# A fused attention and convolution-gate kernel: bias added by the matmul unit, reciprocals folded into the transposes, and eight-plus-eight first taps moved from GpSimd to ScalarE

## Chip, cores and metric

One core of one Trainium2 chip. The metric is the device time of one execution in microseconds. Three executions of the kernel before took 440.35, 440.97 and 441.27 us; their median is 440.97 us.

## What is computed

Attention over 4 batches, 8 heads, 768 positions and head size 64, with eight global keys and a local window of 96 keys behind each query, an ALiBi-like bias, and then a gated feed-forward block on the result:

```python
scores = scale * np.matmul(q, k.transpose(0, 1, 3, 2))
keep = is_global | is_local
bias = -slopes[:, None, None] * dist[None, :, :]
scores = np.where(keep, scores + bias[None, :, :, :], -1000000000.0)
scores = scores - np.max(scores, axis=-1, keepdims=True)
a = np.exp(scores)
a = a / (np.sum(a, axis=-1, keepdims=True) + 1e-09)
x = np.matmul(a, v)                      # then heads side by side: 768 x 512
h = np.maximum(x @ w_in, 0.0)            # 512 -> 1024
conv_out = sum(conv_w[k] * hp[:, k:k + S, :] for k in range(3))
out = (h * (1 / (1 + np.exp(-conv_out)))) @ w_out   # 1024 -> 512
```

## The kernel before, in words

The attention is cut into 32 jobs, one for each batch, half `u` of the 768 positions and pair of heads. A job has three blocks of 128 queries, so there are 96 steps `s`; twelve steps make a half. Each step treats two heads (`j`) and sees 232 gathered keys (128 in the first block of a sequence). A step goes through these stages:

- `scores` (L369): one f32 matmul for each head into one PSUM bank (L381) in the first twelve jobs, that is steps 0 to 35; later jobs use two single-pass matmuls for each head (L391).
- `maxima` (L400): on VectorE, one custom instruction for each head (L408) adds the bias from the bf16 table `tab`, scales, writes the sum back into PSUM and keeps the row extreme; a small accumulator read follows each.
- `exps` (L415): two exponentials on ScalarE (L425) into `pbuf`, with the row sums.
- `normalise` (L433), not in steps 0 to 11, which are scaled later: adds an epsilon, takes a reciprocal on VectorE (L437) and multiplies the 128x232 rows in place, on GpSimd (L443) or partly on ScalarE (L441). In steps 14 to 29 (`alone`) the epsilon (L436) and both multiplications are on GpSimd.
- `transposes` (L445): four PE transposes (L450, L452) with the f32 identity as the moving operand, evacuated by ScalarE (L455).
- `values` or `block`: the value matmuls (L501), then the split into high and low parts (L513, L517).

The feed-forward part of a half (`ffn`, L663) is a queue of items filled in between the steps: 24 `mm1` items (L539), evacuated with a ReLU by ScalarE (L549); the convolution `conv` (L578), whose first tap is a GpSimd multiplication (L585) and whose other two taps are VectorE instructions (L586, L587); the gate (L605, L616), a split (L638 to L641), and `mm2` (L652).

Steps 0 to 13 are ordered by hand (`by_hand`, L792): each engine runs in the order that the code writes, with `warm` filler matmuls on the PE (L168) and one or two pieces of weight decoding on VectorE (L311, L313, L324) for each step. From step 14 the framework orders each engine's instructions itself, from priorities and a cost model, and `fill` (L724) hands out a share of the queue at each step. The weight decoding is spread over steps up to about 30. SP issues the loads, in order.

PSUM has two buffers for scores, two for transposes, one for values and three for the feed-forward products. `setup`, a scratch tile of the start, and the query tiles from job 12 on share one buffer, with the tag `rq`.

Of the kernel before, what the change touches and what calls it, by code (L numbers as in the profile page):

```python
# [9 lines left out]
F32 = mybir.dt.float32  # L10
F32R = mybir.dt.float32r
BF16 = mybir.dt.bfloat16
I32 = mybir.dt.int32
U32 = mybir.dt.uint32
AF = mybir.ActivationFunctionType
ALU = mybir.AluOpType
# [4 lines left out]
P = 128  # L21
# [4 lines left out]
NB = TB // P  # L26
NPREV, NGLOB = 96, 8
WIN = NPREV + P + NGLOB
# [7 lines left out]
NU, SPU = 2 * B, NPAIR * NB  # L36
# [4 lines left out]
HAND = 14  # L41
# [19 lines left out]
def key_start(u, i):  # L61
    return (P + NGLOB) * i - (0 if u or i == 0 else P + NGLOB - 32)
# [5 lines left out]
def fast_path(tc, io):  # L68
    nc = tc.nc
    V, A, G, T = nc.vector, nc.scalar, nc.gpsimd, nc.tensor  # L70
# [4 lines left out]
    def pool(name, bufs, **kw):  # L75
        p = tc.tile_pool(name=name, bufs=bufs, **kw)
        pools.append(p)
        return p.__enter__()

    const = pool("const", 1)  # L80
    p1 = pool("p1", 1)
# [105 lines left out]
    G.iota(keyi, pattern=[[1, 64]], base=0, channel_multiplier=0)  # L187
    ident = const.tile([P, P], F32, name="ident")
    make_identity(nc, ident)
    V.tensor_copy(rel, reli)  # L190
    keepkey = p1.tile([P, NT + 64], F32, tag="ob", name="keep")
    keep, key = keepkey[:, :NT], keepkey[:, NT:]
# [12 lines left out]
    tab = const.tile([P, H, NT], BF16, name="tab")  # L205
# [151 lines left out]
        V.tensor_tensor(bad, bad, red[:, 1:2], ALU.add)  # L357

    steps = [(m, i) for m in range(len(jobs)) for i in range(NB)]
    last_ttr = {}  # L360
    st_s, st_pt, pv, xt, sums = {}, {}, {}, {}, {}

    def alone(s):
        return HAND <= s < NB * (NATIVE - 2)

    def free(s):
        return s < NB * FREE

    def scores(s):  # L369
        m, i = steps[s]  # L370
        b, u, hp = jobs[m]
        w = NKC[u]
        first = u == 0 and i == 0
        n = W0 if first else WIN
        k0 = key_start(u, i)
        both = ps_s.tile([P, 2, 256], F32, tag="s", name=f"s{s}")
        sp = [both[:, 0], both[:, 1]]
        for j in range(2):
            if m < NATIVE:
                rq, rk = raw[m]  # L380
                last_mm[s] = T.matmul(  # L381
                    sp[j][:, :n],
                    rq[:, j, i * P : (i + 1) * P],
                    rk[:, k0 : k0 + n],
                    start=True,
                    stop=True,
                )
                continue
            qh, ql, kk = qk[m]
            for n_, (q_, st, sp_) in enumerate(((qh, True, False), (ql, False, True))):  # L390
                last_mm[s] = T.matmul(  # L391
                    sp[j][:, :n],
                    q_[:, j * TB + i * P : j * TB + (i + 1) * P],
                    kk[:, j * w + k0 : j * w + k0 + n],
                    start=st,
                    stop=sp_,
                )
        st_s[s] = (sp, n, first)

    def maxima(s):  # L400
        m, i = steps[s]
        b, u, hp = jobs[m]
        sp, n, first = st_s[s]
        mm = p1.tile([P, 8], F32, tag="mm", name=f"mm{s}", bufs=6)
        for j in range(2):
            h = 2 * hp + j
            tb = tab[:, h, WIN:] if first else tab[:, h, 0:WIN]
            last_ttr[s] = V.tensor_tensor_reduce(  # L408
                out=sp[j][:, :n], in0=sp[j][:, :n], in1=tb,
                scale=-0.125, scalar=3.0e38, op0=ALU.add, op1=ALU.min,  # L410
                accum_out=mm[:, j : j + 1],
            )
        st_s[s] = (sp, n, mm)

    def exps(s):  # L415
        m, i = steps[s]
        sp, n, mm = st_s[s]
        pb = pbuf[s % NPB]
        total = mm[:, 2:4]
        if free(s):  # L420
            if i == 0:
                sums[m] = p1.tile([P, 4 * NB], F32, tag="sum", name=f"sum{m}", bufs=2)
            total = sums[m][:, 2 * i : 2 * i + 2]
        for j in range(2):
            last_exp[s] = A.activation(  # L425
                pb[:, j * WIN : j * WIN + n], sp[j][:, :n], AF.Exp,
                bias=mm[:, j : j + 1], scale=-1.0, accum_out=total[:, j : j + 1],
            )
        st_s[s] = (pb, n, mm)
        if s < SHARED and not alone(s) and not free(s):  # L430
            A.activation(mm[:, 4:6], mm[:, 2:4], AF.Identity, bias=eps)

    def normalise(s):  # L433
        pb, n, mm = st_s[s]
        if s >= SHARED or alone(s):
            (G if alone(s) else V).tensor_scalar(mm[:, 4:6], mm[:, 2:4], 1.0e-9, 1.0, ALU.add, ALU.mult)  # L436
        V.reciprocal(mm[:, 6:8], mm[:, 4:6])  # L437
        for j in range(2):
            x, inv = pb[:, j * WIN : j * WIN + n], mm[:, 6 + j : 7 + j]
            if j and s < SHARED and not alone(s):  # L440
                A.activation(x, x, AF.Copy, scale=inv)  # L441
            else:
                G.tensor_scalar(x, x, inv, 1.0, ALU.mult, ALU.mult)  # L443

    def transposes(s):  # L445
        m, i = steps[s]
        pb, n, _ = st_s.pop(s)
        pt = ps_t.tile([P, 2, 2, P], F32, tag="t", name=f"t{s}")
        for j in range(2):
            T.transpose(pt[:, 0, j], pb[:, j * WIN : j * WIN + P], ident)  # L450
            if n > P:
                T.transpose(pt[:, 1, j], pb[:, j * WIN + P : j * WIN + 256], ident)  # L452
        sb = p2.tile([P, 2, 2, P], F32, tag="pt", name=f"pt{s}", bufs=NPT)
        k = 2 if n > P else 1
        last_ev[s] = A.activation(sb[:, :k], pt[:, :k], AF.Copy)  # L455
        st_pt[s] = sb
# [121 lines left out]
    def conv(n, f):  # L578
        t0, t1 = bounds[n % 2]
        w = t1 - t0  # L580
        if f == 0:
            cbuf[n] = p1.tile([P, NF, S - CB], F32, tag="c", name=f"c{n}")
        c = cbuf[n][:, f, :w]
        tap = lambda k: (hbuf[:, f, t0 + k : t1 + k], cw[:, k * NF + f : k * NF + f + 1])
        G.tensor_scalar(c, *tap(1), 1.0, ALU.mult, ALU.mult)  # L585
        V.scalar_tensor_tensor(c, *tap(0), c, ALU.mult, ALU.add)  # L586
        V.scalar_tensor_tensor(c, *tap(2), c, ALU.mult, ALU.add)  # L587

# [5 lines left out]
    ready, sure, exact = set(), set(), []  # L594
# [68 lines left out]
    def ffn(n, defer=True):  # L663
# [4 lines left out]
        for f in range(NF):  # L668
            for part in range(3):
                if n or f >= EARLY or not begun[0]:  # L670
                    add(1, mm1, n, f, part)
                elif part == 0:
                    for k in range(begun[0], NK):
                        add(1, mm1_slice, f, k)
                if part == 1:
                    if early:
                        items.append(early.pop(0))
                    if f >= lag:
                        add(0, conv, n, f - lag)
                if part == 2:  # L680
                    g = f - lag + 1
                    if g > 0 and g % WG == 0:
                        add(0, gate, n, g // WG - 1)
                    g -= 1
                    if g > 0 and g % WG == 0:
                        add(0, saturated, n, [g // WG - 1])
        old = tiles_of(n - 1) if n else []
        post = [(0, conv, (n, f)) for f in range(NF - lag, NF)] + [(0, gates, (n,))]
        post += [(0, saturated, (n, range(NG)))]
        post += [(0, split, (n, t)) for t in parts_of(n)]  # L690
# [31 lines left out]
    last_exp, last_mm, last_ev = {}, {}, {}  # L722
# [69 lines left out]
    def by_hand(s):  # L792
        m, i = steps[s]
        p, q = s - 1, s - 2
        scores(s)
        if q >= 0 and free(q):
            block(*steps[q])
# [6 lines left out]
        if p >= 0 and free(p):  # L804
            transposes(p)
        maxima(s)
        exps(s)
        if ends(s - 3):
            mixed_low((s - 3) // NB)
# [5 lines left out]
        if p >= 0 and not free(p):  # L815
            normalise(p)
# [14 lines left out]
    for s in range(len(steps) + LAG_V + 1):  # L831
# [4 lines left out]
        else:  # L836
# [5 lines left out]
            if s < len(steps):  # L842
                scores(s)
                maxima(s)
                exps(s)
# [12 lines left out]
            if s <= len(steps):  # L858
                normalise(s - 1)
# [6 lines left out]
            if s < len(steps) + LAG_T and not free(s - LAG_T):  # L866
                transposes(s - LAG_T)
# [185 lines left out]
def build(nc, io):  # L1053
    with tile.TileContext(nc, schedule_with_timeline_sim=True) as tc:
        fast_path(tc, io)
# [51 lines left out]
```

## Time and profile before

| | |
|---|---|
| median of three executions | 440.97 us |
| the profiled execution | 440.63 us |
| its span, first to last instruction | 438.8 us |
| outside the span | 1.8 us |
| granted TensorE clock | 1.0 of full speed throughout |
| steps 14 to 23, by ScalarE's exponentials | from 45.2 to about 76 us |

Busy times are those of one engine. PE is the matmul unit, PEld its weight loads, which overlap the matmuls, DVE is VectorE, ACT ScalarE, POOL GpSimd. A matmul's end is modelled, so the distance between the starts of two matmuls says more of the PE than the length of either. The chain of waits is followed back from the last instruction: a piece of it is time that, at that moment, the end waited for.

### The profile page before, as it was taken

How to read it: one execution, taken by the hardware profiler on the slowest of the kernel's cores; microseconds unless marked ns; L12 is line 12 of the kernel's file. 1: busy time of each engine (PE TensorE's matmuls, PEld its weight loads, DVE VectorE, ACT ScalarE, POOL GpSimd, SP SyncE). 2: the span in 40 equal slices, each digit the busy share in tenths (PEclk: the TensorE clock that was granted, in tenths of full speed). 3: DMA queues.
4: the chain of work that ended last, by engine and by line, in shares of the span. 5: the costliest groups of instructions: out<-in, count | busy, mean ns of one | idle time of the engine just before them, and what ended most of it. 6: DMA issues, size and time to landing. Idle time of an engine off the chain costs nothing.

```text
span 438.8 us, 10010 instructions
## 1 busy us (share of the span) xinstructions
PE 427.0 (97%) x3566; PEld 404.6 (92%) x3566; DVE 345.1 (79%) x894; ACT 285.2 (65%) x771; POOL 225.4 (51%) x324
## 2 busy tenths in 40 slices
PE   9899979999999999999999999999999999999996
PEld 8677967889999999999999999999999999999996
DVE  6797899979999988767989797867999868556500
ACT  2778688597797866647885767647885866136311
POOL 4312789955735963557668843557668631022000
PEclk9999999999999999999999999999999999999999
DMA  8876864322245234353354224442243467800111
GB/s 256 269 229 183 257 176 154 83 83 91 92 122 160 80 111 136 104 176 94 105 150 152 51 101 134 149 141 85 92 162 120 124 242 240 271 26 0 49 50 55
DMA packets 22570, 58.77 MB, mean 134 GB/s; under 512 B 2928, under 2 KB 6256, under 8 KB 22512
## 3 DMA queue, kind: packets, MB, share of 16 engines
q1 hardware_dynamic: 18608, 51.56, 37.7%
q10 hardware_dynamic: 3904, 6.49, 4.1%
q8 instruction: 30, 0.49, 0.5%
q14 instruction: 28, 0.23, 0.2%
HBM read 51.75 MB, written 6.29 MB: 132 GB/s over the span
## 4 chain that ended last, share of the span: by engine, by line
PE 78%; DVE 12%; ACT 6%; issue 2%; POOL 1%; ACTq 0%; DVEq 0%; POOLq 0%
PE o L652 27%; PE h L539 25%; PE pv L501 7%; PE s L391 5%; PE t L450 4%; PE t L452 3%; DVE s L408 3%; PE s L381 3%; ACT pbuf L425 3%; PE warm L168 2%; DVE c L587 2%; DVE c L586 1%; PE o L922 1%; ACT pt L455 1%; DVE w L313 1%
## 5 line engine op out<-in xcount | busy, mean ns | idle before, releaser
L443 POOL TENSOR_SCALAR pbuf<-pbuf,mm 128x232 f32<-128x232 f32 (+1 forms) x156 | 112.3, 732 | 65.1 <-DVE mm L437 41.0
L425 ACT ACTIVATE pbuf<-s,mm 128x232 f32<-128x232 f32 (+1 forms) x192 | 83.0, 440 | 51.8 <-DVE mm L408 38.1
L408 DVE CUSTOM_DVE_ANT_0 s<-s,tab 128x232 f32<-128x232 f32 (+1 forms) x192 | 73.1, 381 | 9.8 <-PE s L391 4.8
L652 PE MATMUL o<-woh,gh 128*128 128x256 f32 x368 | 77.2, 288 | 0.0
L652 PE MATMUL o<-wol,gh 128*128 128x256 f32 x368 | 76.1, 282 | 0.0
L585 POOL TENSOR_SCALAR c<-hbuf,cw 128x382 f32<-128x382 f32 (+1 forms) x64 | 46.1, 723 | 57.8 <-ACT hbuf L549 55.1
L652 PE MATMUL o<-woh,gl 128*128 128x256 f32 x368 | 72.9, 279 | 0.0
L455 ACT ACTIVATE pt<-t 128x512 f32<-128x512 f32 (+1 forms) x96 | 53.7, 566 | 15.0 <-PE t L452 11.5
L539 PE MATMUL h<-xh,wih 128*128 128x384 f32 x252 | 58.2, 348 | 0.3 <-ACT ob L658 0.2
L539 PE MATMUL h<-xl,wih 128*128 128x384 f32 x252 | 58.0, 345 | 0.0
L652 PEld LDWEIGHTS o<-wol,gh 128*128 128x128 f32 x368 | 57.2, 189 | 0.7
L652 PEld LDWEIGHTS o<-woh,gh 128*128 128x128 f32 x368 | 56.6, 189 | 0.7
L539 PE MATMUL h<-xh,wil 128*128 128x384 f32 x252 | 56.7, 344 | 0.0
L652 PEld LDWEIGHTS o<-woh,gl 128*128 128x128 f32 x368 | 56.2, 189 | 0.1
L586 DVE SCALAR_TENSOR_TENSOR c<-hbuf,cw,c 128x382 f32<-128x382 f32 (+1 forms) x64 | 45.2, 712 | 13.4 <-POOL c L585 13.0
L450 PE MATMUL t<-ident,pbuf 128*128 128x128 f32 x192 | 47.6, 276 | 0.9 <-POOL pbuf L443 0.9
L539 PEld LDWEIGHTS h<-xh,wih 128*128 128x128 f32 x252 | 43.4, 189 | 1.4 <-ACT x L484 0.5
L539 PEld LDWEIGHTS h<-xh,wil 128*128 128x128 f32 x252 | 43.8, 188 | 0.6
L549 ACT ACTIVATE hbuf<-h 128x384 f32<-128x384 f32 x64 | 31.2, 492 | 20.2 <-PE h L539 20.1
L587 DVE SCALAR_TENSOR_TENSOR c<-hbuf,cw,c 128x382 f32<-128x382 f32 (+1 forms) x64 | 43.4, 681 | 0.5
L539 PEld LDWEIGHTS h<-xl,wih 128*128 128x128 f32 x252 | 43.3, 189 | 0.3
L501 PE MATMUL pv<-pt,v 128*64 128x128 f32 (+1 forms) x664 | 40.9, 268 | 0.9 <-ACT pt L455 0.9
(123 smaller groups left out, 844.6 us busy)
## 6 DMA issues: line engine op xcount, KB each, us to landing
v<-in_vv SPq DMA_DIRECT2D x32, 384.0 KB, 3.7
wr<-in_w SPq DMA_DIRECT2D x16, 512.0 KB, 4.4
check<-in_w SPq DMA_DIRECT2D x16, 512.0 KB, 4.1
rq<-in_qk SPq DMA_DIRECT2D x20, 384.0 KB, 3.2
rk<-in_qk SPq DMA_DIRECT2D x12, 504.0 KB, 4.0
out<-ob ACTq DMA_DIRECT2D x23, 256.0 KB, 2.5
rk<-in_qk SPq DMA_DIRECT2D x8, 400.0 KB, 3.6
qz<-in_qt SPq DMA_DIRECT2D x22, 96.0 KB, 4.7
```

The source lines that it names most:

```text
L408: last_ttr[s] = V.tensor_tensor_reduce(out=sp[j][:, :n], in0=sp[j][:, :n], in1=tb, scale=-0.125, scalar=3.0e38, op0=ALU.add, op1=ALU.min, ...
L425: last_exp[s] = A.activation(pb[:, j * WIN : j * WIN + n], sp[j][:, :n], AF.Exp, bias=mm[:, j : j + 1], scale=-1.0, accum_out=total[:, j : ...
L443: G.tensor_scalar(x, x, inv, 1.0, ALU.mult, ALU.mult)
L450: T.transpose(pt[:, 0, j], pb[:, j * WIN : j * WIN + P], ident)
L455: last_ev[s] = A.activation(sb[:, :k], pt[:, :k], AF.Copy)
L501: T.matmul(pv[m][64 * j : 64 * j + 64, i * P + q : (i + 1) * P], vt[m][:n, i, c, 64 * j : 64 * j + 64], sb[:n, c, j, q:], start=c == 0, st ...
L539: T.matmul(ps[:, :TB], w_[:, k, fs], x_, start=part == 0 and k == 0, stop=part == 2 and k == NK - 1,)
L549: A.activation(half, ps[:, :TB], AF.Relu, scale=0.5)
L585: G.tensor_scalar(c, *tap(1), 1.0, ALU.mult, ALU.mult)
L586: V.scalar_tensor_tensor(c, *tap(0), c, ALU.mult, ALU.add)
L587: V.scalar_tensor_tensor(c, *tap(2), c, ALU.mult, ALU.add)
L652: T.matmul(ps[:, c], g_[:, f], w_[:, f, c], start=f == part == k == 0, stop=f == NF - 1 and part == 2 and k == 1,)
```

## The change

Three edits. In steps 3 to 23 the bias table is added in PSUM by a further matmul for each head, with a bf16 identity as the stationary operand; VectorE then takes the row maxima of both heads in one reduction, followed by a small scaling. In steps 14 to 23 the rows of `pbuf` are no longer multiplied: GpSimd multiplies the 128x128 identity by the reciprocals, and the four transposes become ordinary f32 matmuls with that diagonal as the moving operand. In halves 0 and 1 the first tap of the convolution is a ScalarE copy with a scale.

```diff
+    ident16 = const.tile([P, P], BF16, name="ident16")
+    G.tensor_copy(ident16, ident)
...
+    def added(s):
+        return NB <= s < 2 * SPU
+    def spun(s):
+        return HAND <= s < 2 * SPU
...
-                    stop=True,
+                    stop=not added(s),
                 )
+                if added(s):
+                    c0 = WIN if first else 0
+                    last_mm[s] = T.matmul(
+                        sp[j][:, :n], ident16, tab[:, 2 * hp + j, c0 : c0 + n], start=False, stop=True
+                    )
...
+        if added(s):
+            st_s[s] = (sp, n, mm)
+            both = whole.pop(s)
+            V.tensor_reduce(mm[:, 2:4], both[:, :, :n], axis=mybir.AxisListType.X, op=ALU.max)
+            last_ttr[s] = V.tensor_scalar(mm[:, 0:2], mm[:, 2:4], -0.125, None, ALU.mult)
+            return
...
-                bias=mm[:, j : j + 1], scale=-1.0, accum_out=total[:, j : j + 1],
+                bias=mm[:, j : j + 1], scale=0.125 if added(s) else -1.0,
+                accum_out=total[:, j : j + 1],
...
+        if spun(s):
+            if not scale:
+                scale["all"] = p1.tile([P, 3, 2, P], F32, tag="rq", name="scale")
+            scale[s] = scale["all"][:, s % 3]
+            for j in range(2):
+                G.tensor_scalar(scale[s][:, j], ident, mm[:, 6 + j : 7 + j], 1.0, ALU.mult, ALU.mult)
+            return
...
-            T.transpose(pt[:, 0, j], pb[:, j * WIN : j * WIN + P], ident)
-            if n > P:
-                T.transpose(pt[:, 1, j], pb[:, j * WIN + P : j * WIN + 256], ident)
+            for c in range(2 if n > P else 1):
+                x = pb[:, j * WIN + c * P : j * WIN + (c + 1) * P]
+                if spun(s):
+                    T.matmul(pt[:, c, j], x, scale[s][:, j], start=True, stop=True)
+                else:
+                    T.transpose(pt[:, c, j], x, ident)
...
-        G.tensor_scalar(c, *tap(1), 1.0, ALU.mult, ALU.mult)
+        if n < 2 and not exact:
+            A.activation(c, tap(1)[0], AF.Copy, scale=tap(1)[1])
+        else:
+            G.tensor_scalar(c, *tap(1), 1.0, ALU.mult, ALU.mult)
```

## Rows read from the trace of the kernel before

**Rows 1.** The page: weight loads and matmuls in 40 slices, tenths busy.
```profile
PE   9899979999999999999999999999999999999996
PEld 8677967889999999999999999999999999999996
```

**Rows 2.** The page: chain that ended last, share of the span by engine.
```profile
PE 78%; DVE 12%; ACT 6%; issue 2%; POOL 1%; ACTq 0%; DVEq 0%; POOLq 0%
```

**Rows 3.** Busy time by stretch: PE, PEld, DVE, ACT, POOL, then clock and DMA.
```profile
15.00:45.00 30.00, 28.73 (x276) 22.81 (x276) 25.52 (x92) 23.11 (x75) 7.60 (x13) 1.00 0.74 215
45.00:76.00 31.00, 27.93 (x207) 24.75 (x207) 28.94 (x83) 24.75 (x72) 26.76 (x38) 1.00 0.63 198
76.00:92.00 16.00, 14.52 (x110) 12.70 (x105) 14.84 (x46) 10.89 (x39) 15.01 (x26) 1.00 0.37 108
92.00:140.00 48.00, 47.44 (x375) 44.99 (x374) 44.16 (x94) 40.88 (x111) 23.96 (x30) 1.00 0.32 102
200.00:300.00 100.00, 100.00 (x851) 97.07 (x850) 83.49 (x220) 68.37 (x184) 63.59 (x82) 1.00 0.38 117
```

**Rows 4.** Chain of waits, 56 to 76 us: start, length, engine and line.
```profile
59.01 0.78 DVE c L587
59.79 0.88 DVE c L586
60.67 0.32 DVE s L408
60.99 0.06 DVE mm L408
...
61.38 0.60 DVE c L587
```

**Rows 5.** PE in order of time, 61 to 67 us, with waits in brackets.
```profile
63.49 1.05 PE L381 MATMUL s<-rk,qz 128*128 128x232 f32 x4 [1.45 <-ACT pbuf L425]
...
65.93 0.33 PE L452 MATMUL t<-ident,pbuf 128*128 128x128 f32 x1 [0.59 <-POOL pbuf L443]
```

**Rows 6.** Chain of waits in the hand-ordered steps, 7 to 48 us.
```profile
20.27 0.46 PE s L381 x4
20.73 0.62 ACT pt L455
...
22.73 0.35 PE warm L168 x6
...
23.31 0.11 PE t L450
...
31.14 0.79 PE s L381 x4
```

**Rows 7.** Groups by line and shape: count, busy us, mean ns, idle before.
```profile
L408 DVE CUSTOM_DVE_ANT_0 s<-s,tab 128x232 f32<-128x232 f32 x160 | 63.7, 399 | 7.6 <-PE s L391 3.7 <-ACT pt L455 1.4 <-PE s L381 1.0
L408 DVE DVE_READ_ACCUMULATOR2_ANT mm<- 128x1 f32 x192 | 26.4, 137 | 0.1
L349 DVE TENSOR_REDUCE misc<-acc 128x1 f32<-128x512 f32 x1 | 0.7, 685 | 0.0
L242 DVE TENSOR_REDUCE misc<-misc 128x1 f32<-128x3 f32 x1 | 0.2, 157 | 0.0
L436 DVE TENSOR_SCALAR mm<-mm 128x2 f32<-128x2 f32 x56 | 13.9, 248 | 16.8 <-ACT pbuf L425 16.5
L443 POOL TENSOR_SCALAR pbuf<-pbuf,mm 128x232 f32<-128x232 f32 x134 | 100.5, 761 | 47.6 <-DVE mm L437 27.4 <-ACT pbuf L425 8.4 <-ACT pt L455 4.3
L443 POOL TENSOR_SCALAR pbuf<-pbuf,mm 128x128 f32<-128x128 f32 x22 | 11.9, 551 | 17.5 <-DVE mm L437 13.6 <-PE pv L501 1.4 <-PE o L652 1.2
L441 ACT ACTIVATE pbuf<-pbuf,mm 128x232 f32<-128x232 f32 x10 | 4.8, 486 | 0.0
L549 ACT ACTIVATE hbuf<-h 128x384 f32<-128x384 f32 x64 | 31.2, 492 | 20.2 <-PE h L539 20.1
```

**Rows 8.** First tap L585 on POOL by stretch: busy us and count.
```profile
45.00:92.00 47.00, 6.87 (x8) 1.00 0.54 167
92.00:140.00 48.00, 6.90 (x8) 1.00 0.32 102
```

More of the change, by code (lines that the diff above doesn't have):

```diff
@@ L359, in fast_path @@
     steps = [(m, i) for m in range(len(jobs)) for i in range(NB)]
-    last_ttr = {}
+    last_ttr, scale, whole = {}, {}, {}
     st_s, st_pt, pv, xt, sums = {}, {}, {}, {}, {}
+    def added(s):
+        return NB <= s < 2 * SPU
     def alone(s):
         return HAND <= s < NB * (NATIVE - 2)
+    def spun(s):
+        return HAND <= s < 2 * SPU
     def free(s):
@@ L398, in scores @@
         st_s[s] = (sp, n, first)
+        if added(s):
+            whole[s] = both
     def maxima(s):
@@ L404, in maxima @@
         mm = p1.tile([P, 8], F32, tag="mm", name=f"mm{s}", bufs=6)
+        if added(s):
+            st_s[s] = (sp, n, mm)
[3 more added lines that the diff above has]
+            return
         for j in range(2):
```

## The prediction

> **What bounds the kernel now.** I read the page's slices first [rows 1]: from the tenth slice on, the weight loads stand at 9 tenths and the matmuls too; before that the loads dip to 6 to 8 tenths. Then the chain that ended last [rows 2]: 78% of it is PE. So the end is set by the PE's work plus the time in which the PE starved, and the starving lies in the first 140 us.
>
> The table by stretch [rows 3] says how much. Matmul busy time hides short waits, because ends are modelled; the weight loads dip where the waits are, so I measure with them. In the full stretch from 200 to 300 us they are busy 97.07 of 100. By that yardstick, 45 to 76 us could hold 31 x 0.971 = 30.1 us of loads and holds 24.75: 5.35 us of slack. 76 to 92 us: 15.53 - 12.70 = 2.83. 92 to 140 us: 46.6 - 44.99 = 1.6. Together 9.8 us can be won at most behind 45 us, and whatever PE work is added there has to come out of the same 9.8.
>
> Why does it starve between 45 and 76 us? There VectorE is busy 28.94 of 31 us and GpSimd 26.76 [rows 3], the chain runs through VectorE piece after piece [rows 4], and the PE's waits name ScalarE's exponentials (which wait for the maxima) and GpSimd's row multiplications [rows 5]. Two loaded engines feed a PE that is itself nearly loaded. Ahead of 45 us the order is written by hand; the chain [rows 6] passes through PE pieces (transposes, scores, filler) with an evacuation on ScalarE between them.
>
> **Part 1, the bias on the PE, steps 3 to 23.** Added: 21 steps x 2 bf16 matmuls, 232 columns wide (128 in steps 3, 6 and 9). No such matmul is in the trace. The nearest row is the bf16 filler of 128 columns, 0.35 us for 6, 58 ns each [rows 6], a floor. The ceiling is an f32 score instruction of 232 columns, 0.79 us for 4, 197 ns [rows 6]. The filler scaled by 232/128 gives 105 ns, and I take 0.1 us, nearer the filler since both are bf16: 0.2 us a step. That is 2.0 us in steps 14 to 23 (bounds 1.2 to 3.9) and, with three narrow steps at 0.12, 8 x 0.2 + 3 x 0.12 = 2.0 us in steps 3 to 13.
>
> Removed on VectorE: two custom instructions with their reads, 2 x (0.32 + 0.06) = 0.76 us of the chain where another instruction lies between [rows 4], about 1.05 by lengths (2 x (399 + 137) ns, [rows 7]) where they stand next to each other. Added: a reduction of 464 elements. The two reductions in the trace, 685 ns for 512 elements and 157 for 3 [rows 7], give 157 + 461 x 1.037 = 635 ns, and the scaling of two elements is at most 248 ns [rows 7], 0.1 to 0.2 in the chain. About 0.75 to 0.85 us. I take a gain of 0.1 us a step, 1 us over steps 14 to 23; the ends are nothing and 0.25 us a step. The Trainium skill (VectorE: DVE Perf Modes, Rules for kernel authors) speaks against this exchange: a reduction runs at one element per cycle, is called the slowest VectorE operation, and one is told to keep the count of operations low. The row agrees as to the rate (1.04 ns an element), and by that rule alone VectorE's term would be 0 in place of 1 us.
>
> In the hand-ordered steps the 2.0 us are not all on the path. Of steps 4 to 13, seven (4 to 10) have their scores in the PE part of the chain: 5 x 0.2 + 2 x 0.12 = 1.2 us. At two of them the next thing is a wait for an evacuation that is late for another reason (0.62 us of L455 behind 0.46 us of scores, [rows 6]), so about 0.4 is absorbed. Behind the matmul that waits or lengthens, the PE queue holds value matmuls and filler. VectorE's earlier end gives back 0.2. Sum: +0.6 us (bounds -0.5 and +2.0). The identity's bf16 copy on GpSimd is one 128x128 operation, at most 0.55 us [rows 7]; it stands ahead of GpSimd's wait for VectorE's first distances and costs nothing; without that cover, 0.55. The bias table becomes an operand of the PE rather than of VectorE; it is written two or more steps ahead, so no new wait.
>
> **Part 2, the diagonal, steps 14 to 23.** Removed on GpSimd: 20 multiplications at 761 ns; added: 20 at 551 (same operation, 128 columns, [rows 7]): -4.2 us. On the PE, a transpose is one instruction, 0.11 us [rows 6]; an f32 matmul is two, as the four score instructions of a step with two heads show: 128 columns take 0.46 / 4 = 0.115 each [rows 6]. So four transposes go from 0.44 to 0.88-0.92 us: +0.44 a step, **+4.4 us** over ten steps. This term has a narrow bound (4 to 5). The reciprocal tile shares the buffer of `rq`: its first write waits for readers of step 6, long past; the query load of job 12, on SP, waits for step 23's transposes but is issued only in step 31. No DMA is added.
>
> **Part 3, the first tap.** 16 GpSimd instructions go, 6.87 us in 45 to 92 and 6.90 in 92 to 140 us [rows 8]. 16 ScalarE copies come. Nearest rows: the scaled copy of 232 columns, 486 ns, and a ReLU of 384 columns, 492 ns [rows 7]; between 0.49 and 0.62 us each, I take 0.5 net of overlap: 4 us in each of the two stretches. ScalarE is busy 24.75 + 10.89 of 47 us and 40.88 of 48 [rows 3]; it rises to 39.6 of 47 and 44.9 of 48. No queue is at its limit, so I cost it at nothing on its own; the cover is thin in the second stretch (rival 2).
>
> **The sum.** PE work added between 45 and 76 us: 2.0 + 4.4 = 6.4 us. Slack there: 5.35. GpSimd loses about a third of its load and VectorE about 1 us, so most starving should go, but the added work exceeds the slack: the PE becomes the bound of these ten steps. I let it recover 4.3 of 5.35 there, 0.7 of 2.83 in 76 to 92 us (whose waits follow from GpSimd's arrears) and nothing after. Net: 6.4 - 5.0 = +1.4. With the hand-ordered +0.6 and 0.2 for ScalarE: **+2.2 us**. Against the profiled execution's own 440.63 us (span 438.8 plus 1.83 around it): 442.8 us. That execution lies 0.3 us below the median of three, so against the median it is +1.9.
>
> **Rival 1: faster, because the feeding engines were the real limit.** The same VectorE instruction takes 0.60 us in one place and 0.78 in another, its neighbour 0.88 [rows 4], while GpSimd was busy 26.76 of 31 us [rows 3]. If those lengths come from the two working at once, taking 6.87 + 4.2 us off GpSimd shortens some 25 VectorE instructions by up to 0.2 us each, and all starving behind 45 us but 1 us is won: 6.4 - 8.8 = -2.4, +0.6 by hand: 438.8 us. It decides once recovery passes 7 us. The Trainium skill (GPSIMD Engine Reference, Specifications) has such a rule: GpSimd's way into SBUF is shared with VectorE, with contention when a VectorE instruction reads two SBUF inputs, as the two later taps do. By that rule, which the two lengths bear out, the time is this rival's. Against it: the recovery would have to reach stretches that the added work does not touch. Chance 0.25.
>
> **Rival 2: ScalarE takes over.** Between 92 and 140 us ScalarE has the exponentials, evacuations, ReLUs and gates of a half, and 44.9 of 48 us would be full. A tap between a ReLU and the next exponential delays that exponential by 0.5 us; if half of the 16 do, +4 less what the forecast holds for it: 446.6 us. For it: the waits for exponentials [rows 5]. Against: the PE has a backlog of feed-forward work there, and its loads are near the yardstick. Chance 0.13.
>
> **Rival 3: the parts cancel.** Recovery of 6 to 7 us pays for the added 6.4 and the hand-ordered 0.6: 440.1 to 441.8 us, 440.9 in the middle. Chance 0.17. That the edits don't do what they say I can't construct; the shared buffer is the only place for it.
>
> **Numbers.** A measurement of this kernel can tell about 0.2%, 0.9 us, from no change. Forecast 442.8 us, chance 0.45 (441.9 to 445). Faster 0.25, within 0.2% 0.17, slower 0.45 + 0.13 = 0.58. The range runs from 438.4 (rival 1 with a little more) to 446.6 (rival 2), leaving out about 0.1 on each side; the bias price's bounds (-1 to +3 us about the forecast, [rows 6]) lie inside. The slower cases alone: 441.9 to 446.6.
>
> **What would show it.** Right: in the ten steps the weight loads rise from 0.80 of the time to 0.93 or more, GpSimd falls to about half, the chain there turns from VectorE to PE, four diagonal transposes take 0.9 us, a bias matmul 0.1, and the steps end 1 to 3 us later than at 76 us. Wrong: the chain stays on VectorE with the loads still at 0.8; step 24 begins before 75 us; ScalarE over 0.93 busy with the PE waiting for it; or a bias matmul at 0.2 us.

## The result, and the profile after

Five executions of the changed kernel have a median of 443.64 us (443.32 to 444.49), five of the kernel before 440.46 us. The ratio is 1.0075 [1.0064, 1.0085]: slower by about 3.2 us, inside the range, 0.84 us above the forecast. The profiled execution took 443.32 us, its span 441.4 against 438.8.

The page of the changed kernel: busy times, the slices that answer to [rows 1], and the shares of the chain that answer to [rows 2].

```profile
PE 432.4 (98%) x3648; PEld 410.7 (93%) x3648; DVE 341.3 (77%) x852; ACT 291.8 (66%) x787; POOL 212.1 (48%) x309
PE   9999999999999999999999999999999999999996
PEld 8777998889999999999999999999999999999996
PE 80%; DVE 6%; DMA 5%; ACT 4%; issue 2%; POOL 2%; ACTq 0%; POOLq 0%; DVEq 0%
```

VectorE's share of the chain halves, from 12% to 6%, and PE's grows by 2 points, to 80%. A DMA share of 5% is new; it is taken up below.

By stretch, the changed kernel, columns as in [rows 3]; the stretches are moved by one to three microseconds so that they hold the same steps:

```profile
46.00:78.00 32.00, 32.00 (x260) 29.26 (x260) 27.82 (x66) 27.06 (x79) 21.46 (x36) 1.00 0.57 174
78.00:94.00 16.00, 14.57 (x110) 12.74 (x106) 13.80 (x45) 11.48 (x38) 10.97 (x21) 1.00 0.46 133
94.00:143.00 49.00, 49.00 (x388) 47.30 (x386) 43.85 (x101) 46.48 (x128) 20.48 (x21) 1.00 0.35 102
```

In the first stretch the loads rise from 0.80 to 29.26 / 32 = 0.91, GpSimd falls from 0.86 to 0.67 and VectorE from 0.93 to 0.87. In the second, where no PE work was added, the loads are as before (12.74 of 16 us against 12.70). ScalarE is fullest in the third, 0.95, but the PE's loads there are at 47.30 / 49 = 0.965, close to the yardstick of 0.971: it has work to put before the exponentials.

The changed kernel's PE in order of time, in one of the ten steps:

```profile
60.12 0.66 PE L389 MATMUL s<-rk,qz 128*128 128x232 f32 x2
60.61 0.26 PE L398 MATMUL s<-tab,ident 128*128 128x232 bf16 x1
60.71 0.57 PE L389 MATMUL s<-rk,qz 128*128 128x232 f32 x2
61.11 0.26 PE L398 MATMUL s<-tab,ident 128*128 128x232 bf16 x1
61.21 1.07 PE L482 MATMUL t<-scale,pbuf 128*128 128x128 f32 x8
```

Read the starts, not the lengths. A bias matmul at 61.11 is followed at 61.21: 0.10 us, as costed. One diagonal transpose is two instructions. And the chain of the changed kernel for the same ten steps, which answers to [rows 4]:

```profile
61.38 0.90 PE t L482 x8
62.28 0.69 PE h L571 x4
62.97 0.89 PE t L482 x8
...
67.36 0.11 PE s L398
67.50 0.64 DVE mm L423
68.38 1.66 POOL scale L465 x2
70.12 0.20 POOL mm L458
70.35 0.17 DVE mm L459
70.52 0.88 DVE c L621
```

Eight diagonal instructions take 0.89 to 0.90 us, against 0.44 for four transposes: the 0.44 us a step of the prediction. Up to 67 us the chain is on the PE, as forecast; from there on it runs through VectorE and GpSimd. The PE does not starve beside it in these steps: it is busy 31.45 of 31.45 us (row under e5). What this part of the chain leads to lies behind step 24, where the PE is busy 14.99 of 16.42 us (77.58 to 94.00).

Groups of the changed kernel by shape, which answer to [rows 7] and [rows 8]:

```profile
L423 DVE TENSOR_REDUCE mm<-s 128x2 f32<-128x464 f32 x18 | 11.4, 634 | 4.0 <-PE s L398 4.0
L424 DVE TENSOR_SCALAR mm<-mm 128x2 f32<-128x2 f32 x21 | 3.7, 176 | 0.5
L465 POOL TENSOR_SCALAR scale<-ident,mm 128x128 f32<-128x128 f32 x20 | 15.3, 775 | 4.4 <-DVE mm L459 3.0 <-PE t L482 0.7 <-DVE mm L424 0.7
L618 ACT ACTIVATE c<-hbuf,cw 128x382 f32<-128x382 f32 x8 | 4.9, 631 | 0.0
L398 PEld LDWEIGHTS <-ident 128*128 128x128 bf16 x42 | 4.1, 98 | 0.2
```

The reduction takes 634 ns (635 estimated) and the scaling 176. The diagonal's multiplication takes 775 ns, not 551. The prices of GpSimd in these steps, 45 to 77 us before and 45 to 78 after, are:

```profile
L443 POOL TENSOR_SCALAR pbuf<-pbuf,mm 128x232 f32<-128x232 f32 x17 | 14.3, 854 | 0.3
```

```profile
L465 POOL TENSOR_SCALAR scale<-ident,mm 128x128 f32<-128x128 f32 x19 | 15.0, 797 | 4.4 <-DVE mm L459 3.0 <-PE t L482 0.7 <-DVE mm L424 0.7
```

The replaced multiplication took 854 ns here, not the 761 of the whole kernel, so an instruction saves about 0.06 to 0.08 us in place of 0.21. GpSimd is relieved almost by the taps alone. A tap on ScalarE takes 631 ns, a little above the bracket of 0.49 to 0.62.

**Where the 2.6 us of span arise.** Four marks cut the execution: an exponential of the hand-ordered start (at 13.80 us before, 13.84 after), the first of step 14, the first of step 57, and the start of ScalarE's last evacuation (L926 before, L961 after); the end is that of the last instruction, 438.83 and 441.43 us. Before / after:

| stretch | before | after | difference |
|---|---|---|---|
| start mark to step 14 | 31.44 | 32.29 | +0.85 |
| step 14 to step 57 | 158.95 | 159.58 | +0.63 |
| step 57 to the last evacuation | 231.04 | 232.11 | +1.07 |
| last evacuation to the end | 3.61 | 3.61 | 0 |

The first two terms are those that the prediction has. The third it has not. The chain of the changed kernel there:

```profile
359.39 1.02 DVE acc L344
360.42 0.02 issue
360.44 4.44 DMA check<-in_w
364.87 0.02 issue
364.90 0.70 DVE acc L344
365.60 0.02 issue
365.62 4.52 DMA check<-in_w
370.14 0.03 issue
...
370.24 0.69 DVE acc L344
370.93 1.15 DVE c L673
```

These are the loads (16 of 512 KB) of weight words whose top bits VectorE gathers into `acc` (L341, L344), for the choice between this program and its general branch; a further load is issued when an earlier one has been read. The gate's split (L673) stands behind the last of them on VectorE. In the kernel before the chain of this stretch is on the PE throughout.

### The profile page after: what moved, and what is told of

It is laid out like the page before. It is cut to its first block, busy times and chain, and to the rows that moved or that the text cites. A ratio compares the mean times of both kernels' runs of the same rounds, so it can differ in the third digit from the quotient of the medians.

```text
span 441.4 us, 10130 instructions
## 1 busy us (share of the span) xinstructions
PE 432.4 (98%) x3648; PEld 410.7 (93%) x3648; DVE 341.3 (77%) x852; ACT 291.8 (66%) x787; POOL 212.1 (48%) x309
## 4 chain that ended last, share of the span: by engine, by line
PE 80%; DVE 6%; DMA 5%; ACT 4%; issue 2%; POOL 2%; ACTq 0%; POOLq 0%; DVEq 0%
PE h L571 26%; PE o L687 25%; PE pv L533 7%; PE t L484 6%; PE s L404 5%; DMA check<-in_w 5%; PE s L389 4%; PE warm L168 2%; ACT pbuf L446 2%; PE o L957 1%; DVE s L429 1%; PE t L482 1%; DVE c L621 1%; ACT pt L487 1%; POOL scale L465 1%
## 5 line engine op out<-in xcount | busy, mean ns | idle before, releaser
L472 POOL TENSOR_SCALAR pbuf<-pbuf,mm 128x232 f32<-128x232 f32 (+1 forms) x136 | 98.1, 732 | 76.0 <-DVE mm L459 53.0
L429 DVE CUSTOM_DVE_ANT_0 s<-s,tab 128x232 f32<-128x232 f32 (+1 forms) x150 | 56.9, 382 | 9.5 <-PE s L404 7.5
L620 POOL TENSOR_SCALAR c<-hbuf,cw 128x382 f32<-128x382 f32 (+1 forms) x48 | 32.5, 679 | 54.3 <-ACT hbuf L581 33.1
L621 DVE SCALAR_TENSOR_TENSOR c<-hbuf,cw,c 128x382 f32<-128x382 f32 (+1 forms) x64 | 45.2, 709 | 10.6 <-POOL c L620 9.8
L484 PE MATMUL t<-ident,pbuf 128*128 128x128 f32 x312 | 50.7, 274 | 0.8 <-ACT pt L487 0.4
L533 PEld LDWEIGHTS pv<-pt,v 128*64 128x64 f32 (+1 forms) x664 | 34.0, 136 | 9.4 <-ACT pt L487 4.6
```

Of the source, the lines that this page charges most:

```text
L429: last_ttr[s] = V.tensor_tensor_reduce(out=sp[j][:, :n], in0=sp[j][:, :n], in1=tb, scale=-0.125, scalar=3.0e38, op0=ALU.add, op1=ALU.min, ...
L484: T.transpose(pt[:, c, j], x, ident)
L533: T.matmul(pv[m][64 * j : 64 * j + 64, i * P + q : (i + 1) * P], vt[m][:n, i, c, 64 * j : 64 * j + 64], sb[:n, c, j, q:], start=c == 0, st ...
```

## The experiments

Each kernel ran beside the kernel before on the same chip. The table gives the differences from the kernel before, in us: the stretches from each kernel's profiled execution, the last column from the medians. "Recovered" is the PE work added in steps 14 to 23, at 0.2 us a step for the bias and 0.44 for the diagonal, less the difference of step 14 to 57 (in e11 1.1 us come on top for steps 24 to 26, of which step 24 is narrow); it is what came, on balance, out of the pool of starved time that the prediction put at 9.8 us.

| kernel | PE work added | to step 14 | 14 to 57 | recovered | 57 to last evacuation | last evacuation to end | median |
|---|---|---|---|---|---|---|---|
| changed | 6.4 | +0.85 | +0.63 | 5.8 | +1.07 | 0 | +3.2 |
| e1, taps | 0 | +0.01 | -1.02 | 1.0 | 0 | 0 | -0.9 |
| e2, bias | 2.0 | +0.84 | +0.70 | 1.3 | -0.15 | +0.47 | +2.2 |
| e3, diagonal | 4.4 | +0.01 | -0.93 | 5.3 | +0.58 | +0.91 | +1.0 |
| e4, all but bias by hand | 6.4 | -0.02 | +0.68 | 5.7 | 0 | 0 | +0.9 |
| e5, taps and diagonal | 4.4 | 0 | -3.02 | 7.4 | 0 | +1.30 | -1.8 |
| e6, bias by hand | 0 | +0.84 | -0.21 | 0.2 | 0 | 0 | +0.8 |
| e7, three check loads | 6.4 | +0.83 | +0.69 | 5.7 | 0 | +0.36 | +2.1 |
| e8, bias twice | 8.4 | +0.86 | +1.33 | 7.1 | -0.30 | 0 | +2.7 |
| e9, zero matmuls on e5 | 6.4 | -0.02 | -0.54 | 6.9 | 0 | +0.13 | -0.2 |
| e10, reduction on e5 | 4.4 | +0.20 | -4.44 | 8.8 | +0.20 | +1.03 | -3.3 |
| e11, e5 to step 26 | 5.5 | 0 | -0.91 | 6.4 | 0 | 0 | -0.8 |
| e12, e5 with half 0's taps | 4.4 | +0.02 | -2.05 | 6.5 | 0 | +1.77 | -0.5 |

The four stretches add up to the median's difference within 0.4 us, but for e8 (0.8 off) and the changed kernel (0.6); of both the profiled execution is the fastest of five, 0.4 and 0.3 us under its median.

**Parts alone.** All edits are against the changed kernel. e1 keeps the taps only:

```diff
 def added(s):
-    return NB <= s < 2 * SPU
+    return False
...
 def spun(s):
-    return HAND <= s < 2 * SPU
+    return False
```

> Only the first tap of halves 0 and 1 moves to ScalarE; bias and transposes as before. Theory (the cost is added PE work, the taps only relieve GpSimd and VectorE): no PE work is added, so the time falls by 0.5 to 2 us against before, and the steps behind 45 us end earlier. Rival (ScalarE takes over between 92 and 140 us): slower than before by 1 to 4 us. Rival (taps don't matter): within 0.5 us.

439.35 us, ratio 0.9978 [0.997, 0.9987]. The taps gain 0.9 us, as expected, and by the traces all of it in the ten steps (30.55 to 29.56 us). Two views of the kernel before and of this one show where: VectorE's two later taps, from 45 to 92 us, first before and then e1.

```profile
L586 DVE SCALAR_TENSOR_TENSOR c<-hbuf,cw,c 128x382 f32<-128x382 f32 x8 | 6.0, 748 | 0.7 <-POOL c L585 0.7
L587 DVE SCALAR_TENSOR_TENSOR c<-hbuf,cw,c 128x382 f32<-128x382 f32 x8 | 5.7, 716 | 0.0
```

```profile
L621 DVE SCALAR_TENSOR_TENSOR c<-hbuf,cw,c 128x382 f32<-128x382 f32 x8 | 5.5, 682 | 0.3 <-ACT c L618 0.3
L622 DVE SCALAR_TENSOR_TENSOR c<-hbuf,cw,c 128x382 f32<-128x382 f32 x8 | 5.5, 686 | 0.1
```

The same instructions are 30 to 66 ns shorter with less work on GpSimd. That agrees in direction with the rule behind rival 1 (the Trainium skill, GPSIMD Engine Reference, Specifications), at a third, at most, of the 0.2 us that the rival let each instruction save.

e2 keeps the bias only:

```diff
 def spun(s):
-    return HAND <= s < 2 * SPU
+    return False
...
-        if n < 2 and not exact:
+        if False:
```

> Only the bias on the PE in steps 3 to 23. Theory (PE work): step 14 is later by 0.9 us as in the changed kernel; in steps 14 to 23 another 2.0 us of PE work meet 5.35 us of slack and a VectorE that has 1 us less, so -0.5 to +1 us there: 0.4 to 1.9 us slower than before in all. Rival (VectorE was the real limit): at least 0.5 us faster than before.

442.41 us, 1.0048 [1.0034, 1.0061]: +0.84 ahead of step 14 and +0.70 behind it. Alone, 2.0 us of PE work find 1.3. At 2.2 us over before it is a little outside the 0.4 to 1.9 expected; the stretch to step 57 is inside, and 0.47 us come behind the last evacuation.

e3 keeps the diagonal only:

```diff
 def added(s):
-    return NB <= s < 2 * SPU
+    return False
...
-        if n < 2 and not exact:
+        if False:
```

> Only the diagonal reciprocals in steps 14 to 23. Theory (PE work): 4.4 us of PE work meet 5.35 us of slack of which GpSimd's relief opens only a part: 0.5 to 2.5 us slower than before; step 14 unmoved. Rival (GpSimd was the real limit): 0.5 us or more faster.

441.16 us, 1.002 [1.0011, 1.003]. By the table its 4.4 us of PE work cost nothing up to step 57, which comes 0.9 us earlier; the loss is behind the last evacuation and in the late stretch, whose chain holds check loads here too (3.85 and 4.60 us). So the total fell into the range expected, but for another reason than PE work.

**The hand-ordered steps.** e4 takes the bias matmul out of them:

```diff
 def added(s):
-    return NB <= s < 2 * SPU
+    return HAND <= s < 2 * SPU
```

> The changed kernel with the bias on the PE in steps 14 to 23 alone; steps 3 to 13 as before. Theory: step 14's first exponential stands at 45.2 us again, and the time is 0.9 us under that of the changed kernel, some 2.3 us over before. Rival (what happens ahead of 45 us is absorbed later): no difference from the changed kernel, 3.2 us over before.

441.14 us, 1.0024 [1.0014, 1.0034]. That is 2.3 us less than the changed kernel's +3.2, where 0.9 was expected: the late stretch's +1.07 went with the hand-ordered +0.85.

e6 has it there and nothing else of the change:

```diff
 def added(s):
-    return NB <= s < 2 * SPU
+    return NB <= s < HAND
...
 def spun(s):
-    return HAND <= s < 2 * SPU
+    return False
...
-        if n < 2 and not exact:
+        if False:
```

> Only the bias on the PE, and only in steps 3 to 13. Theory (a shift of the hand-ordered part runs through to the end, plus what the late check loads add): step 14 later by 0.85 us, 0.85 to 2.2 us slower than before. Rival (the bias in steps 14 to 23 is what costs): under 0.5 us slower.

441.17 us, 1.0019 [1.0011, 1.0028], just under the 0.85 us expected at least. The two runs agree on the hand-ordered part: 0.84 us ahead of step 14 in e6, nothing in e4. Of it 0.63 us last to the final evacuation of e6. e4's late stretch is that of the kernel before to 0.01 us, so the third term of the result is not the ten steps' doing by itself; nor is it the hand-ordered steps', as e6 has none of it.

**The base without the bias matmuls.** e5 has the diagonal and the taps.

```diff
 def added(s):
-    return NB <= s < 2 * SPU
+    return False
```

> The changed kernel without the bias on the PE: taps on ScalarE and the diagonal. Theory (parts add up: taps -0.9 us, diagonal +0.9 us against before): within 0.5 us of before. Rival (both open the same slack, so the second brings nothing and the diagonal's PE work stays): 1 to 2 us slower than the taps alone, that is 0 to 1 us slower than before, with step 24 later than with the taps alone. Rival (steps 48 and later stood 0.9 to 1 us earlier with either, and that adds): 1.5 us faster than before up to 340 us.

438.63 us, 0.996 [0.9948, 0.9973], faster than both kernels. The parts were expected to add up, within 0.5 us of before: a miss. What came is the rival in which more than the parts is won. Steps 14 to 57 lose 3.02 us, more than e1 and e3 together (1.95). Busy time from the first exponential of step 14 to that of step 24, of the kernel before, the changed one and e5, in this order:

```profile
45.24:75.79 30.55, 27.48 (x201) 24.30 (x201) 28.49 (x83) 24.30 (x72) 26.55 (x38) 1.00 0.63 198
```

```profile
46.13:77.58 31.45, 31.45 (x250) 28.71 (x251) 27.27 (x65) 26.51 (x76) 21.04 (x36) 1.00 0.58 176
```

```profile
45.30:75.86 30.56, 30.52 (x245) 29.16 (x244) 27.88 (x83) 26.47 (x77) 18.45 (x34) 1.00 0.60 182
```

In e5 the ten steps hold 4.86 us more of loads than before in the same 30.55 us: the loads are busy 0.954. So the diagonal's whole 4.4 us went into starved time, and the 3 us come behind step 24. With the bias matmuls the ten steps last 0.9 us longer. Their loads are busy 0.913, but the PE is as full as in e5, 31.45 of 31.45 us against 30.52 of 30.56: behind a bias matmul's load (0.10 us from 60.92) the next starts only at 61.12, while the matmuls follow each other without a gap.

**The late stretch.** e7 loads three of the sixteen blocks of check words and reads the same three again; the check of the other thirteen is left out.

```diff
-        x = words[k]
+        x = words[k % 3]
...
-        if len(words) < NCHK:
-            check_load()
```

> The changed kernel, but the check of the weights' range looks at 3 of its 16 pieces five times over: the VectorE instructions stay, 13 late loads of 256 KB go. Theory (about 1.1 us of the loss arises between 345 and 373 us, where VectorE waits for check loads): 1.0 to 1.5 us faster than the changed kernel, 1.7 to 2.2 us slower than before. Rival (those waits are covered and the loss is the PE's): no difference from the changed kernel.

442.45 us, 1.0045 [1.0032, 1.0058], 1.2 us under the changed kernel, as expected (the loads left out are of 512 KB, not 256). Its chain in the same stretch:

```profile
363.06 0.59 PE o L685 x5
363.64 1.35 PE pv L531 x24
365.00 3.15 PE o L685 x25
```

PE throughout, and the stretch from step 57 to the last evacuation is 231.04 us again, as before. The third term is the check loads. Why they are exposed in the changed kernel and in e3 and not in e4, e5 or e6, which have all sixteen, is open.

**More PE work, and the bias taken apart.** e8 adds to the changed kernel, in steps 14 to 23, one more bf16 matmul for each head, which adds zeros:

```diff
-                        sp[j][:, :n], ident16, tab[:, 2 * hp + j, c0 : c0 + n], start=False, stop=True
+                        sp[j][:, :n], ident16, tab[:, 2 * hp + j, c0 : c0 + n], start=False, stop=not spun(s)
                     )
+                    if spun(s):
+                        nil = pbuf[0][:, 2 * WIN : 2 * WIN + 1].bitcast(BF16)[:, 0:1]
+                        last_mm[s] = T.matmul(
+                            sp[j][:, :n], ident16, nil.to_broadcast([P, n]), start=False, stop=True
+                        )
```

> The changed kernel with another 20 bf16 matmuls of 232 columns in steps 14 to 23, which add zeros: 2.0 us of PE work more at 0.1 us each. Theory (the PE bounds these ten steps after the change): 1.5 to 2.5 us slower than the changed kernel. Rival (there is still slack in them): less than 0.7 us slower.

443.07 us, 1.006 [1.0047, 1.0073], which overlaps the changed kernel's interval. A miss: 2.0 us more of PE work made steps 14 to 57 only 0.70 us longer, so the changed kernel still had starved time left. It was not in the ten steps: these grew by 0.66 us (31.45 to 32.11), the PE busy throughout in both. The stretch behind them kept its length (128.13 and 128.17 us) and holds 0.74 us more of loads (121.13 and 121.87): work that the ten steps had no room for moved there.

e9 puts those matmuls of zeros into e5, where VectorE still adds the bias:

```diff
 def added(s):
-    return NB <= s < 2 * SPU
+    return False
...
-                if added(s):
-                    c0 = WIN if first else 0
+                if spun(s):
+                    nil = pbuf[0][:, 2 * WIN : 2 * WIN + 1].bitcast(BF16)[:, 0:1]
...
-                        sp[j][:, :n], ident16, tab[:, 2 * hp + j, c0 : c0 + n], start=False, stop=True
+                        sp[j][:, :n], ident16, nil.to_broadcast([P, n]), start=False, stop=True
```

> Taps and diagonal as in the fifth experiment (438.6 us), VectorE's maxima as before, and in steps 14 to 23 one bf16 matmul of 232 columns more for each head, which adds zeros: the bias's PE work without its exchange on VectorE. Theory (2.0 us of added PE work that no slack is left for): 1.5 to 2.5 us slower than the fifth experiment. Rival (the exchange on VectorE delays the exponentials, the PE work is hidden): within 0.5 us of the fifth experiment.

440.13 us, 1.0004 [0.9992, 1.0016]: 1.5 us over e5 by medians, 2.48 in steps 14 to 57. On e5, 2.0 us of PE work are paid in full and a little over, as expected.

e10 puts the reduction and the scaling into e5 without the matmuls; the bias of steps 14 to 23 is left out:

```diff
 def added(s):
-    return NB <= s < 2 * SPU
+    return HAND <= s < 2 * SPU
...
-                if added(s):
-                    c0 = WIN if first else 0
-                    last_mm[s] = T.matmul(
-                        sp[j][:, :n], ident16, tab[:, 2 * hp + j, c0 : c0 + n], start=False, stop=True
-                    )
```

> Taps and diagonal as in the fifth experiment, and in steps 14 to 23 VectorE's one reduction and scaling in place of the two custom instructions, but no bias matmul: the bias of these steps is left out. Theory (PE work is what costs): 0 to 1 us faster than the fifth experiment. Rival (the exchange on VectorE delays the exponentials): 1.5 to 3 us slower than the fifth experiment.

437.04 us, 0.9918 [0.9906, 0.9931]: 1.6 us under e5, where 0 to 1 was expected; 1.42 of it in steps 14 to 57. VectorE's exchange of two custom instructions for one reduction is a gain, and a larger one than the 1.0 us taken. The Trainium skill (VectorE: DVE Perf Modes, Rules for kernel authors) calls a reduction the slowest VectorE operation, which speaks against it. The two instructions that came take 634 + 176 ns, the four that went 2 x (399 + 137) ns [rows 7]; the exchange as a whole does not cost, and the measurement decides.

The reduction's idle time in the ten steps, in the changed kernel and in e10:

```profile
L423 DVE TENSOR_REDUCE mm<-s 128x2 f32<-128x464 f32 x9 | 5.7, 632 | 3.1 <-PE s L398 3.1
```

```profile
L418 DVE TENSOR_REDUCE mm<-s 128x2 f32<-128x464 f32 x9 | 5.7, 634 | 1.5 <-PE s L389 1.5
```

**Two sizes of e5.** e11 carries its diagonal on to step 26:

```diff
 def spun(s):
-    return HAND <= s < 2 * SPU
+    return HAND <= s < 27
```

> The fifth experiment with the diagonal in steps 14 to 26: 1.1 us of PE work more, two thirds of GpSimd's row multiplications of three steps less. Theory (the diagonal pays for itself wherever the PE waits for GpSimd, and some 1.5 us of slack is left between steps 24 and 31): within 0.7 us of the fifth experiment. Rival (no slack is left): 1.1 us slower or more.

439.56 us, 0.9982 [0.9973, 0.9991], 0.9 us over e5, for 0.22 + 2 x 0.44 = 1.1 us of PE work; in steps 14 to 57 it is 2.11, of which the shorter end gives back 1.3. Within 0.7 us was expected: a miss. Behind step 23 the added work finds no room.

e12 leaves half 1's taps on GpSimd in e5:

```diff
-        if n < 2 and not exact:
+        if n < 1 and not exact:
```

> The fifth experiment with the first tap of half 1 back on GpSimd; that of half 0 stays on ScalarE. Theory (the PE starves mostly ahead of 92 us, where half 0's taps lie): within 0.5 us of the fifth experiment. Rival (half 1's taps, between 92 and 140 us, are worth as much): 0.5 to 1.2 us slower. Rival (ScalarE is short of time there): 0.5 us or more faster.

439.87 us, 0.9982 [0.9974, 0.9991], 1.2 us over e5; in steps 14 to 57 it is 0.97. That is the rival (0.5 to 1.2), not the theory: half 1's taps carry a part of the gain although the PE is near its yardstick there. The intervals of e11 and e12 begin where that of e5 ends.

## Why the prediction was right, and where it was not

**Half of the mechanism stands.** The PE became the bound of the ten steps, the hand-ordered part was paid, and step 24 began 1.79 us later (75.79 to 77.58), within the 1 to 3 foreseen; 0.89 of that is the shift of step 14. A bias matmul took 0.10 us and four diagonal transposes 0.9. The loads reached 0.91, short of 0.93, because a bias matmul's load is short (98 ns) and the next does not follow at once: twenty gaps of about 0.1 us are 2 us of 31.45. GpSimd fell to 0.67, not to about half, and the chain turned to the PE in part. The other half, a cost made of the PE work that exceeds the slack, does not stand: the diagonal's 4.4 us, with the taps, left the kernel faster than before (e5), the changed kernel still had room for more (e8), and the loss behind step 14 lies with the bias.

**That 443.64 comes so near to 442.8 is luck in part:** two errors of about 1 us, below, nearly cancel.

**Hand-ordered steps:** +0.6 forecast, +0.85 measured, and repeated in e2, e6, e7 and e8 (0.83 to 0.86).

**Steps 14 to 57:** +1.6 forecast (+1.4, and 0.2 for ScalarE), +0.63 measured: 5.8 us recovered where 5.0 were taken. The size that was off is the recovery, and its place: the ten steps grew by 0.90 us (30.55 to 31.45), so they recovered 5.5 us and not 4.3; behind step 24 the changed kernel won 0.27 (128.40 to 128.13 us) and not 0.7. Without the bias matmuls the whole 4.4 us of the diagonal found room in the ten steps, and behind step 24 e5 won 3.0 us (75.86 to 201.23 us, for 75.79 to 204.19).

**ScalarE's +0.2 had the wrong sign.** The taps gain 0.9 us by themselves. Rival 2 falls: ScalarE reached 0.95, above the 44.9 of 48 us that it named, and the PE did not starve.

**GpSimd's -4.2 us did not come in the changed kernel.** Both prices [rows 7] were taken from other steps than those in which they were paid: 854 ns before and 775 to 797 in the changed kernel make about 1.1 to 1.6 us for twenty. In e5 the instruction took 626 ns, in e9, which has the matmuls without VectorE's exchange, 607, and in e10, which has the exchange without the matmuls, 607. Of these kernels it is over 0.7 us only where both stand together; what lengthens it there was not tested.

**A term was missing:** +1.07 us from the check loads, which were hidden before. Within the span the sum is 0.85 + 0.63 + 1.07 = 2.55, against 2.2 forecast: -1.0 behind step 14 and +1.1 in the late stretch nearly cancel. e7 shows the check loads to be the cause.

**Rival 1 was right about the pool and wrong about the change.** e5 recovers 7.4 us and e10 8.8, the figure that the rival used. Its mechanism is shown for a small part at most: in e1 VectorE's later taps are 8 x (66 + 30) ns = 0.8 us shorter. The bias keeps the changed kernel from such a recovery. Step 14 to 57, e5 to e4, is 3.70 us longer; of that, the PE work of two matmuls a step is 2.48 (e9) and the VectorE exchange -1.42 (e10). Some 2.6 us belong to the two together. By stretch, steps 24 to 57 of e4 and then of e5:

```profile
76.31:204.50 128.19, 126.26 (x1042) 121.15 (x1037) 109.75 (x281) 98.95 (x278) 69.94 (x95) 1.00 0.37 112
```

```profile
75.86:201.23 125.37, 124.83 (x1026) 119.81 (x1025) 109.57 (x282) 98.92 (x279) 75.98 (x97) 1.00 0.38 115
```

Only 0.88 of the 3.70 us lie in the ten steps, where the PE is full in both; 2.82 lie behind, where no bias matmul runs: 1.34 us more of loads, work moved out of the ten steps, and PE idle time of 1.93 us for 0.54. What makes the PE idle there is not shown. The reduction of both heads has to wait for the last bias matmul, 3.1 us against 1.5 for the scores, which may be the start of it. That is argued: from step 14 on the framework orders the instructions anew for each kernel, and no run held the order fixed.

## What to carry to other kernels

Count the bound engine's starved time by stretch and lay added work against that pool: within it the work can be free, as the diagonal's 4.4 us were in e5's ten steps. The size of the pool alone does not give the price: another 2.0 us cost 2.48 on e5 (e9) and 0.70 on the changed kernel (e8). Take an instruction's price from the steps in which it will run. Run parts alone and in pairs, since here neither gains nor costs added up: taps -0.9 and diagonal +1.0 gave -1.8 together, and the bias that looked like VectorE relief cost more than the PE time it took (3.65 us for 2.0 in steps 14 to 57). The version to keep is e5, the taps and the diagonal with the bias left on VectorE, at 0.996 [0.9948, 0.9973].

## What was not expected of the hardware

The stretch from the last evacuation to the end, one 128 KB store, is not constant: 3.60 or 3.61 us in six of these kernels and in the one before, 3.7 to 4.1 in e2, e7 and e9, 4.52 in e3, 4.64 in e10, 4.91 in e5 and 5.37 in e12, with the same instructions ahead of it. The table's sums come nearer to the medians with it, which speaks against an accident of one execution; it takes 1.3 of the 3.0 us that e5 had won.

The traces show what goes with it. The store lands 1.7 us after its issue in the kernel before and 3.0 in e5. A packet of 16 KB on the queue that the page calls `q8 instruction`, one of 30 in the kernel before, lies near it, and its place differs from kernel to kernel:

| kernel | 16 KB packet ends | store's last packet ends | end of the program |
|---|---|---|---|
| before | 0.27 | 1.37 | 3.19 |
| e9 | 0.69 | 1.39 | 3.32 |
| e2 | 1.03 | 1.73 | 3.67 |
| e3 | 1.47 | 2.16 | 4.10 |
| e10 | 1.59 | 2.29 | 4.22 |
| e5 | 1.81 | 2.56 | 4.49 |
| e12 | 2.33 | 3.02 | 4.96 |

All times are us after the issue of the last store. In e3, e5, e10 and e12, 135 of the store's 144 packets have ended by 1.37, as all have in the kernel before; the other nine, a sixteenth, end one after the other behind the 16 KB packet, the last some 0.7 us after it, and the program 1.9 us after that. So one of the sixteen DMA engines' shares of the store came late behind that transfer (that the nine belong to one engine is inferred from their number). e7 is an exception: its store is not late (1.37), and its +0.36 stays open. No run moved the packet; this is read from the traces and not tested.
